# Pooled attention and a top-1 mixture of experts on one core: second products turned by TensorE for four parts, first V loads behind Q, later landings in the planner's model, one outer condition

## The chip, the cores and the metric

The kernel runs on one core of a Trainium2 chip. The core has five engines that run in parallel, each in its own order: TensorE (PE, matrix products and transposes), VectorE (DVE), ScalarE (ACT), GpSimd (POOL) and SyncE (SP, which here only issues transfers). Transfers run on DMA engines, and engines wait for one another and for transfers by semaphores. The metric is the time of one execution on the device in microseconds (us).

## The reference

```python
q_pool = q.reshape(B, H, S // 2, 2, D).mean(axis=3)
scores = scale * np.matmul(q_pool, k.transpose(0, 1, 3, 2))
attn = softmax(scores)
x = np.matmul(attn, v).transpose(0, 2, 1, 3).reshape(N, 512)

expert_idx = np.argmax(x @ w_gate, axis=1)
gate_w = softmax(x @ w_gate)[np.arange(N), expert_idx]
for e in range(8):
    mask = expert_idx == e
    h = np.maximum(x[mask] @ w1[e], 0.0)
    out[mask] = gate_w[mask, None] * (h @ w2[e])
```

The sizes are B = 8 batches, H = 8 heads, S = 1152 positions and D = 64 features a head, in fp32. Pooling leaves 576 rows of Q a batch, so N = 4608 tokens of 512 features go to the experts. w1 is 512 x 1024 for each expert and w2 is 1024 x 512. A token goes to one expert only.

## The kernel before, in words

**A planner.** `Flow` collects steps (`add`, an engine, a cost, a key, the steps it comes after, the buffers it holds) and `emit` simulates them once, when the program is built: a free engine takes the ready step with the smallest key. The key is a due time in units of the products; the constants `K_LOAD` to `K_SLOT` and `AHEAD` shift the keys of one kind of step. `carry` (L115 on) is a step that issues a transfer, together with a step on a modelled DMA that takes `move` ns, and `late` ns more until others may go on. These numbers change only the order. Each engine then executes in the order found; DVE, for instance, never lets a later instruction pass one that waits. Gathers and scatters are `paced`: such a transfer gets a dependence on PE's instruction before it in the order.

**Attention.** A batch is four pairs of heads. `load_pair` (L456) loads K, Q (two overlapping transfers) and V of a pair on SP (L472), pools Q (`qp`, L479, on POOL; for the very first pair on DVE) and turns K and Q on PE (L500, L506). `scores` (product L544) and `values` (L648) follow, with the exponent on ACT (L577). POOL adds the exponentials up in folds of 3.9 us (L623), and PE finishes the sums (L632). PE works in tile modes there (`ROWS`, `QUADS`, `COLS`), and changing the mode costs something. K, Q have one buffer each, V has three.

**Routing.** After each batch the router (L711 on) chooses experts; `enlist` (L825, POOL) scatters (token, weight) records to lists in memory, one per expert.

**The experts.** Tokens of an expert are worked on in 15 parts of 160 to 416 tokens: two early ones of 384 that start within the last batch, and those of `RANKS`, ordered by size of the expert. The parts of 288 tokens are r0's second and r4's first, those of 320 and of 416 are r3's first and r5. A part loads its list (`li`, L910, POOL), makes an index from it on DVE (`ix`, L920), gathers rows of x in blocks of 32 tokens (`xr`, `xq`, L926, POOL), weighs and turns them (`turn_tokens`: DVE L1083, L1084, L1087) and splits them in a high and a low half (`xh` on ACT L1091, `xl` on DVE L1046). Weights are split likewise (`w1h`, `w2h` on ACT L1108, `w1l`, `w2l` on DVE L1046). Every fp32 product is three fp32r products: high by high, low by high, high by low. `first_products` (L1140) leave the hidden rows turned (1024 features on partitions by tokens), in halves `hh` (ACT L1147) and `hl` (DVE L1149). In `second_products` hidden rows of a block of up to 128 tokens are stationary and w2 moves:

```python
for r in range(x.nr):
    for k, (a, b) in enumerate(((hh, wh), (hh, wl), (hl, wh))):
        made = nc.tensor.matmul(py.t[:n], a[:, c, hs], b[:, c % 2, :], ...)
```

That is 24 products of 512 columns for each block (L1170), whether it has 128 tokens or the last 32. ACT copies the block (L1188) and POOL scatters its rows to the output (L1178).

**The end.** Two conditions stand behind the planned part, each read by every engine from a small table on the core (`stab`): a fallback `If` (load L1263, branch L1265), which is taken only when a list overflows, and a loop over slots left over (load L1282, loop L1290), which has no pass for these inputs.

Of the kernel before, what the change touches and what calls it, by code (L numbers as in the profile page):

```python
# [42 lines left out]
K_FIRST = 29  # L43
K_PUT = 79
K_SPREAD = -1
K_NEXT = 38
TABLE_OPS = 3
K_TAB = 1
K_SLOT = 46
# [6 lines left out]
AHEAD = 216  # L56
# [209 lines left out]
def kernel(  # L266
# [148 lines left out]
    def open_attention(exact, base, pairs, units):  # L415
# [10 lines left out]
        o.turned = []  # L426
# [28 lines left out]
    def done(*steps):  # L455
        return [s for s in steps if s is not None]  # L456

    def load_pair(o, f, key, b, hp):
# [15 lines left out]
        q0 = f.carry("SP", 960, lambda: [load(qn.t[i * D:(i + 1) * D], qb[i * BL:i * BL + D]) for i in range(2)],  # L474
                     key + K_LOAD, (), [qn], 2600)
        x.v = f.carry("SP", 480, lambda: load(vn.t, heads(v, b, hp).rearrange("h (p c) d -> p h c d", p=P)),
                    key + (-30 if opening else K_V), (), [vn], 2600)
# [216 lines left out]
    def routing(o, f, key, b, xT, rec, sums, ready, hold=()):  # L694
# [144 lines left out]
        for j in range(NJ):  # L839
            outs.append(f.carry("POOL", 1230, lambda j=j: enlist(j), at + (K_PUT if b is None or b < B - 2 else 0) * j / NJ, done(p, *hold), [di, re], 40, 2400, paced=CALM))  # L840
# [49 lines left out]
    def tokens_of(o, f, key, tab, s, n, known, stored, early=False, m=None):  # L890
# [47 lines left out]
    def slot_table(o, f, key, ready, later=None):  # L938
# [81 lines left out]
        flush()  # L1020
        return known

    def flag(o, f, key, ready):
# [5 lines left out]
        for fn in (  # L1029
            lambda: nc.vector.tensor_reduce(f2, pm.t[0:1, :QP], axis=AX.X, op=ALU.max),  # L1030
            lambda: nc.vector.tensor_scalar(f3[:, 0:1], f2, 1.0, None, op0=ALU.is_le),
            lambda: nc.vector.tensor_scalar(stab[:, 1:2], f3[:, 0:1], -1.0, 1.0, op0=ALU.mult, op1=ALU.add),
        ):
            p = f.add("DVE", 100, fn, key, done(p), [pm])

# [119 lines left out]
    def second_products(o, m, f, x, key):  # L1155

        for r in range(x.nr):
            py = hold_of("py", lambda h: m.ps.tile([P, DM], F32, **h.own("py")))
# [4 lines left out]
            for c0 in range(0, NFC, 2):  # L1163
# [29 lines left out]
    with ExitStack() as cm, ExitStack() as units, ExitStack() as pairs:  # L1193
# [48 lines left out]
        for i, ns in enumerate(((EARLY_N,),) * EARLY + RANKS):  # L1242
# [3 lines left out]
            for j, n in enumerate(ns):  # L1246
# [7 lines left out]
                if j == 0:  # L1254
# [8 lines left out]
    again = nc.values_load(stab[0:1, 1:2], min_val=0, max_val=1,  # L1263
                           skip_runtime_bounds_check_because="a comparison's result")
    with tc.If(again > 0):  # L1265
        reset_state()
        empty_lists()
        with ExitStack() as cm:
            o = open_attention(True, cm, cm, cm)
            with tc.For_i(0, B, 1) as b:  # L1270
# [6 lines left out]
                for hp in range(NHP):  # L1277
                    attend(o, f, 0, b, hp, xT, sums, [])
# [47 lines left out]
```

## Time and profile before

| | before |
|---|---|
| median of three runs | 1222.98 us (1222.68 to 1224.88) |
| the profiled execution's own time | 1222.86 us |
| its span in the trace | 1221.3 us |
| mean granted clock of TensorE | 0.984 |
| busy: PE, weight loads | 1169.4 us (96%), 826.4 us (68%) |
| busy: DVE, ACT, POOL | 781.7, 629.7, 854.4 us |

The span is the time from the first to the last instruction in the trace; the execution's own time is taken around it. A busy engine is one whose instructions run; the time of instructions that issue, wait or branch does not count. The chain of waits follows the work that ended last back to the start. Attention takes about 12 to 735 us in the trace, the experts 735 to 1208, and the end the rest.

### The profile page before, as it was taken

The page shows a single profiled execution, that of the slowest core. Times are in us where ns is not written, and L with a number is a line of the kernel's source. Part 1 is how long each engine was busy: PE and PEld are TensorE (multiplying, and loading weights), DVE is VectorE, ACT ScalarE, POOL GpSimd, SP SyncE. Part 2 cuts the span into 40 slices and gives each one's busy share as a digit, 9 for nine tenths or more (in the row PEclk, how much of TensorE's full clock was granted, in tenths as well). Part 3 has the DMA queues.
Part 4 walks back from the last instruction along what each step waited for, and adds up shares of the span by engine and source line. Part 5 has one row for each costly group of instructions (what it writes and reads, how often), then busy time and mean ns, then how long its engine had stood idle before and what let it go on. Part 6 is the DMA issues. An engine that isn't in the chain of part 4 may idle for free.

```text
span 1221.3 us, 33596 instructions
## 1 busy us (share of the span) xinstructions
PE 1169.4 (96%) x14061; PEld 826.4 (68%) x14061; DVE 781.7 (64%) x2145; ACT 629.7 (52%) x768; POOL 854.4 (70%) x468
## 2 busy tenths in 40 slices
PE   7999999999999999999999998799999999999995
PEld 3555565566566566565665556688898888989784
DVE  5767777777777777778668658764546363636440
ACT  3676567666667567567666456341424141425340
POOL 2999899899899899899999153465666564630110
PEclk8999999999999999999999998899999998999998
DMA  7643333433523524524433315743434361615310
GB/s 196 157 119 88 103 104 88 123 95 96 124 84 102 126 77 112 126 83 113 109 93 117 108 48 169 184 141 96 130 118 141 104 187 37 193 45 185 121 63 19
DMA packets 76049, 138.10 MB, mean 113 GB/s; under 512 B 9833, under 2 KB 33265, under 8 KB 75888
## 3 DMA queue, kind: packets, MB, share of 16 engines
q1 hardware_dynamic: 65088, 116.18, 34.3%
q0 software_dynamic: 9712, 19.64, 5.5%
q8 instruction: 113, 1.85, 0.7%
q14 instruction: 48, 0.39, 0.1%
q10 hardware_dynamic: 1088, 0.03, 0.1%
HBM read 115.04 MB, written 21.02 MB: 111 GB/s over the span
## 4 chain that ended last, share of the span: by engine, by line
PE 78%; POOL 6%; DVE 5%; issue 4%; DMA 4%; ACT 2%; POOLq 0%; SPq 0%; DVEq 0%
PE st L544 19%; PE m L648 18%; PE py L1170 17%; PE ph L1140 15%; POOL fold L623 5%; PE sums L632 3%; DVE s L549 2%; PE st L500 2%; PE sums L618 1%; POOL lists L825 1%; ACT s L577 1%; DMA xr<-x_runs,ix 1%; PE st L506 1%; DMA lists<-re,di 1%; DMA xq<-x_runs,ix 1%
## 5 line engine op out<-in xcount | busy, mean ns | idle before, releaser
L549 DVE TENSOR_SCALAR_CACHE_REDUCE s<-st 128x576 f32<-128x576 f32 x576 | 421.0, 753 | 161.2 <-PE st L544 155.7
L577 ACT ACTIVATE s<-s,bias 128x1728 f32<-128x1728 f32 x192 | 321.4, 1730 | 177.9 <-DVE bias L573 156.4
L544 PE MATMUL st<-qT,kT 64*64 64x288 f32 x4608 | 372.3, 410 | 9.9 <-DVE s L549 6.7
L648 PE MATMUL m<-s,vn 64*64 64x288 f32 x4608 | 363.2, 405 | 0.0
L544 PEld LDWEIGHTS st<-qT,kT 64*64 64x64 f32 x4608 | 169.5, 133 | 140.0 <-DVE s L549 57.0
L648 PEld LDWEIGHTS m<-s,vn 64*64 64x64 f32 x4608 | 182.1, 133 | 84.6 <-ACT xT L653 2.6
L623 POOL TENSOR_TENSOR fold<-s 128x1728 f32<-128x1728 f32 x58 | 224.5, 3871 | 9.1 <-ACT s L577 8.4
L623 POOL TENSOR_TENSOR fold<-fold,s 128x1728 f32<-128x1728 f32 x58 | 224.9, 3877 | 1.6
L926 POOL DMA_INDIRECT xr<-x_runs,ix x99 | 113.8, 1149 | 91.5 <-PE ph L1140 24.5
L1140 PE MATMUL ph<-xh,w1h 128*128 128x384 f32 (+6 forms) x480 | 152.5, 318 | 17.8 <-DVE hl L1149 15.0
L1140 PE MATMUL ph<-xl,w1h 128*128 128x384 f32 (+6 forms) x480 | 151.0, 315 | 0.5 <-DVE xl L1046 0.5
L1140 PE MATMUL ph<-xh,w1l 128*128 128x384 f32 (+6 forms) x480 | 150.5, 313 | 0.0
L1178 POOL DMA_INDIRECT out_dram<-y,rec x41 | 45.7, 1114 | 143.7 <-PE py L1170 79.6
L1170 PE MATMUL py<-w2h,hh 128*128 128x512 f32 (+1 forms) x328 | 129.6, 395 | 0.0
L1170 PE MATMUL py<-w2h,hl 128*128 128x512 f32 (+1 forms) x328 | 129.3, 394 | 0.0
L1170 PE MATMUL py<-w2l,hh 128*128 128x512 f32 (+1 forms) x328 | 128.9, 393 | 0.0
L1147 ACT ACTIVATE hh<-ph 128x384 fp32r<-128x384 f32 (+5 forms) x100 | 48.7, 487 | 149.4 <-PE ph L1140 147.1
L1149 DVE SCALAR_TENSOR_TENSOR hl<-ph,hh 128x384 fp32r<-128x384 f32 (+5 forms) x100 | 54.6, 549 | 91.8 <-ACT hh L1147 91.7
L1140 PEld LDWEIGHTS ph<-xh,w1h 128*128 128x128 f32 x480 | 92.4, 193 | 22.0 <-DVE hl L1149 17.2
L1140 PEld LDWEIGHTS ph<-xl,w1h 128*128 128x128 f32 x480 | 92.3, 192 | 1.8 <-DVE xl L1046 0.9
L1140 PEld LDWEIGHTS ph<-xh,w1l 128*128 128x128 f32 x480 | 92.0, 192 | 0.0
L1188 ACT COPY y<-py 128x512 f32<-128x512 f32 (+3 forms) x41 | 24.0, 586 | 124.0 <-PE py L1170 114.7
(174 smaller groups left out, 1331.5 us busy)
## 6 DMA issues: line engine op xcount, KB each, us to landing
raw<-in_moe_w_dram SPq DMA_DIRECT2D x80, 512.0 KB
qn<-in_q_dram SPq DMA_DIRECT2D x64, 384.0 KB
kn<-in_k_dram SPq DMA_DIRECT2D x32, 576.0 KB
vn<-in_v_dram SPq DMA_DIRECT2D x32, 576.0 KB
x_runs<-row SPq DMA_DIRECT2D x24, 396.0 KB
xr<-x_runs,ix POOLq DMA_INDIRECT x99, 2.7
x_runs<-empty SPq DMA_DIRECT2D x4, 297.0 KB
xq<-x_runs,ix POOLq DMA_INDIRECT x49, 2.9
```

Source lines behind the costliest of these rows:

```text
L544: made = nc.tensor.matmul(pt.t[to, h, :HQ], x.kT.t[up, c * P + i * D:c * P + (i + 1) * D], x.qT.t[up, cols], start=True, stop=True, tile_p ...
L549: nc.vector.tensor_scalar(s.t[:, c], pt.t[:, :, :HQ], -SCALE, None, op0=ALU.mult, op1=ALU.min, accum_out=mx.t[:, c:c + 1],)
L577: nc.scalar.activation(s.t[:, c0:c0 + n], s.t[:, c0:c0 + n], AF.Exp, bias=bias.t, scale=-1.0)
L623: add = lambda to, a, b: nc.gpsimd.tensor_tensor(to, a, b, ALU.add)
L632: nc.tensor.matmul(sums.t[to, :HQ], ones4[:, hp, half, :], u.t[:, i, h], start=hp == half == 0, stop=hp == NHP - 1 and half == 1, tile_pos ...
L648: made = nc.tensor.matmul(pa[i].t[cs, :HQ], x.vn.t[up, h, c, :], s.t[up, c, h], start=c == 0, stop=c == NC - 1, tile_position=(up.start, c ...
L926: return nc.gpsimd.indirect_dma_start(out=x.xr[i // NQD].t[:, i % NQD, :], out_offset=None, in_=xg, in_offset=bass.IndirectOffsetOnAxis(ap ...
L1140: made = nc.tensor.matmul(view()[:, i, :], a[:, c, fp], b[:, c, :n], start=c == 0 and k == 0, stop=c == NDC - 1 and k == 2)
L1147: a = f.add("ACT", act(nb * n) - 44, lambda fs=fs, view=view: nc.scalar.activation(hidden(m)[0][:, fs, :n], view(), AF.Relu), at - 20, don ...
L1149: d = f.add("DVE", dve(nb * n), lambda fs=fs, view=view: nc.vector.scalar_tensor_tensor(hidden(m)[1][:, fs, :n], view(), 0.0, hidden(m)[0] ...
L1170: made = nc.tensor.matmul(py.t[:n], a[:, c, hs], b[:, c % 2, :], start=c == 0 and k == 0, stop=c == NFC - 1 and k == 2)
L1178: ins = nc.gpsimd.indirect_dma_start(out=out, out_offset=bass.IndirectOffsetOnAxis(ap=x.re.t[:up, r:r + 1], axis=0), in_=y.t[:up], in_offs ...
```

## The change

1. Fourteen constants of the planner are set anew.
2. The V loads of batch 0 get a dependence on both Q loads of their pair, so SP waits there until Q has landed. Later V loads come after the V load before them in the plan (a planner's rule alone).
3. The model lets the scatters of `enlist`, the loads of lists and the gathers land 2000 or 3000 ns later.
4. Parts with more than 256 tokens whose last block has 32 or 64 (288, 320, 288 and 416) take their second products the other way: a 128 x 128 piece of w2 is stationary and the hidden rows of all tokens move. The result is 4 groups of 128 output features by tokens; ACT copies each to `yT`, PE turns it back in 128 x 128 transposes (fp32, L1205 of the changed kernel), then ACT's copy and the scatter follow as before.
5. The two conditions at the end stand inside one outer `If`, on the sum of the flag and the slots (`stab[2]`), which two small instructions on DVE work out.

```diff
-K_LOAD = -65
-K_V = -40
-K_POOL = -16
-K_PIECE = -28
-K_TOP = -8
+K_LOAD = -57
+K_V = -36
+K_POOL = -7
+K_PIECE = -26
+K_TOP = -17
...
-K_EXP = 10
+K_EXP = 13
...
-K_ROW = 34
+K_ROW = 47
...
-K_FIRST = 29
-K_PUT = 79
-K_SPREAD = -1
-K_NEXT = 38
+K_FIRST = 37
+K_PUT = 88
+K_SPREAD = 4
+K_NEXT = 41
...
-K_TAB = 1
-K_SLOT = 46
+REST = (32, 64)
+K_TAB = 0
+K_SLOT = 45
...
-AHEAD = 216
+AHEAD = 270
...
+        first = not o.exact and b == 0
...
+        def load_v():
+            ins = load(vn.t, heads(v, b, hp).rearrange("h (p c) d -> p h c d", p=P))
+            if first:
+                for other in x.q_loads:
+                    tc.add_manual_dep(ins.ins, other.ins.name, mybir.DependencyInfo(
+                        mybir.DependencyClass.Sync, mybir.DependencyReason.DATA), reason="Q is needed sooner")
...
+        x.v = f.carry("SP", 480, load_v, key + (-30 if opening else K_V), done(q0) if first else done(o.before), [vn], 2600)
+        o.before = x.v
...
-            outs.append(f.carry("POOL", 1230, lambda j=j: enlist(j), at + (K_PUT if b is None or b < B - 2 else 0) * j / NJ, done(p, *hold), [di, re], 40, 2400, paced=CALM))
+            outs.append(f.carry("POOL", 1230, lambda j=j: enlist(j), at + (K_PUT if b is None or b < B - 2 else 0) * j / NJ, done(p, *hold), [di, re], 40, 4400, paced=CALM))
...
-        p = f.carry(at, 900 if early else 1100, load, key - LEAD, [*known, *stored], [x.re, x.li], 120, 9000 if early else 1000)
+        p = f.carry(at, 900 if early else 1100, load, key - LEAD, [*known, *stored], [x.re, x.li], 120, 9000 if early else 4000)
...
-        x.rows = done(*(f.carry("POOL", 1310, lambda i=i: gather(i), key + i * 3 / x.nb, done(p, *stored), [x.ix, x.xr[i // NQD]], 400, paced=CALM if early else CALM_X)
+        x.rows = done(*(f.carry("POOL", 1310, lambda i=i: gather(i), key + i * 3 / x.nb, done(p, *stored), [x.ix, x.xr[i // NQD]], 400, 2000, paced=CALM if early else CALM_X)
...
+        n, across = x.n, f.room is not None and x.n > 2 * P and x.of[-1] * BL in REST
+        if across:
+            yT = tile_of(o, "xT", [P, NHP, NQ])
+            turned = []
+            for d in range(NDC):
...
+                        for c in (c0, c0 + 1):
+                            for k, (a, b) in enumerate(((wh, hh), (wl, hh), (wh, hl))):
+                                made = nc.tensor.matmul(py.t[:, :n], a[:, c % 2, ds], b[:, c, :n],
+                                                        start=c == 0 and k == 0, stop=c == NFC - 1 and k == 2)
...
+                turned.append(f.add("ACT", act(n) - 44, lambda d=d, py=py: nc.scalar.copy(yT.t[:, d, :n], py.t[:, :n]),
+                                    at, done(p), [py, yT]))
...
+            if across:
+                def product(r=r, py=py, up=up):
+                    for d in range(NDC):
+                        made = nc.tensor.transpose(py.t[:up, d * P:(d + 1) * P], yT.t[:, d, r * P:r * P + up], ident)
+                    return made
+
+                p = f.add("PE", 60 * NDC, product, at + 40, turned, [py, yT])
...
+    some = nc.values_load(stab[0:1, 2:3], min_val=0, max_val=MAXS + 1,
+                          skip_runtime_bounds_check_because="a comparison's result and the sum of the slots")
+    with tc.If(some > 0):
```

The order of the instructions moves in many places. Three are shown, with the names of the programs (a number behind a name tells buffers apart).

First DVE, at the start of the parts of `RANKS`, around the index of the first list (`ix_2`, read from `li_2`); `hl` are the low halves of the hidden rows of the second early part. Before:

```order
L1046 TENSOR_TENSOR w2l1_10642<-raw_1_10439,w2h1_10641 128x1024
L920 TENSOR_SCALAR ix_2_10670<-li_2_10599,gid_147 128x12
L923 COPY rec2_2_10672<-li_2_10599 32x3 x4
L1046 TENSOR_TENSOR w2l2_10662<-raw_2_10557,w2h2_10661 128x1024
L1046 TENSOR_TENSOR w2l3_10694<-raw_3_10570,w2h3_10693 128x1024
L1149 SCALAR_TENSOR_TENSOR hl_10296<-ph_0_10677,hh_10295 128x384
```

and in the changed kernel, with the table of slots (L966, L1049) between:

```order
L1061 TENSOR_TENSOR w2l3_10681<-raw_3_10570,w2h3_10680 128x1024
L1046 TENSOR_SCALAR f3_221<-f3_221 1x1
L1164 SCALAR_TENSOR_TENSOR hl_10298<-ph_0_10671,hh_10297 128x384
L966 TENSOR_TENSOR t_rf_217<-t_rf_217,t_sT_218 1x25
L966 CAST stab_175<-t_cum_213 1x1
L1164 SCALAR_TENSOR_TENSOR hl_10298<-ph_1_10700,hh_10297 128x384
L932 TENSOR_SCALAR ix_2_10750<-li_2_10622,gid_147 128x12
L935 COPY rec2_2_10752<-li_2_10622 32x3 x4
```

The index moved from ahead of two weight halves and the first `hl` to behind the second.

Second DVE again, where the first ranked part (384 tokens) begins: its first block `xr_0` is weighed and turned, and the low halves of the expert's w2 are made beside it. Before:

```order
L1083 TENSOR_TENSOR xr_0_10910<-xr_0_10910,li_2_10599 128x4x4
L1084 TENSOR_TENSOR xr_0_10910<-xr_0_10910 128x4x128
L1087 STREAM_TRANSPOSE xt_0_11014<-xr_0_10910 128x4x4x32
L1046 TENSOR_TENSOR xl_10923<-xt_0_11014,xh_10922 128x4x128
L1046 TENSOR_TENSOR w2l0_11024<-raw_2_10708,w2h0_11023 128x1024
L1046 TENSOR_TENSOR w2l1_11038<-raw_3_10730,w2h1_11037 128x1024
L1046 TENSOR_TENSOR w2l2_11058<-raw_4_10796,w2h2_11057 128x1024
L1046 TENSOR_TENSOR w2l3_11076<-raw_5_10846,w2h3_11075 128x1024
L1149 SCALAR_TENSOR_TENSOR hl_10296<-ph_0_11063,hh_10295 128x384
```

and in the changed kernel:

```order
L1061 TENSOR_TENSOR w2l0_11018<-raw_2_10696,w2h0_11017 128x1024
L1061 TENSOR_TENSOR w2l1_11031<-raw_3_10715,w2h1_11030 128x1024
L1061 TENSOR_TENSOR w2l2_11046<-raw_4_10787,w2h2_11045 128x1024
L1098 TENSOR_TENSOR xr_0_10943<-xr_0_10943,li_2_10622 128x4x4
L1099 TENSOR_TENSOR xr_0_10943<-xr_0_10943 128x4x128
L1061 TENSOR_TENSOR w2l3_11057<-raw_5_10849,w2h3_11056 128x1024
L1102 STREAM_TRANSPOSE xt_0_11069<-xr_0_10943 128x4x4x32
L1061 TENSOR_TENSOR xl_10941<-xt_0_11069,xh_10940 128x4x128
L1098 TENSOR_TENSOR xr_1_11007<-xr_1_11007,li_3_10638 128x4x4
L1099 TENSOR_TENSOR xr_1_11007<-xr_1_11007 128x4x128
L1164 SCALAR_TENSOR_TENSOR hl_10298<-ph_0_11082,hh_10297 128x384
```

Three of the four weight halves moved from behind the weighing of `xr_0` to ahead of it, and the fourth between weighing and turning.

Third PE, at the end of the second products of r0's part of 288 tokens (`py` is the last of the four groups of output features, `m` the banks that take the transposes, `ph` the next part's first products). Before, after 24 products of one block came 24 of the next:

```order
L1170 MATMUL py_0_11599<-w2h3_11075,hh_10295 128x512
L1170 MATMUL py_0_11599<-w2l3_11076,hh_10295 128x512
L1170 MATMUL py_0_11599<-w2h3_11075,hl_10296 128x512
L1170 MATMUL py_1_11648<-w2h0_11023,hh_10295 128x512
L1170 MATMUL py_1_11648<-w2l0_11024,hh_10295 128x512
```

and in the changed kernel:

```order
L1186 MATMUL py_0_11680<-hh_10297,w2h3_11056 128x288
L1186 MATMUL py_0_11680<-hh_10297,w2l3_11057 128x288
L1186 MATMUL py_0_11680<-hl_10298,w2h3_11056 128x288
L1155 MATMUL ph_0_11720<-xh_11570,w1h0_11427 128x384
L1155 MATMUL ph_0_11720<-xl_11571,w1h0_11427 128x384
L1155 MATMUL ph_0_11720<-xh_11570,w1l0_11428 128x384
L1205 MATMUL m_0_11736<-ident_64,xT_0_11605 128x128 x4
L1205 MATMUL m_2_11744<-ident_64,xT_0_11605 128x128 x4
```

The products have 288 columns in place of 512; six first products of the next part stand between the last of them and the eight transposes of two blocks, and the third block's four follow later.

## Rows read from the trace of the kernel before

**Rows 1.** Windows: busy us (PE, PEld, DVE, ACT, POOL), clock, DMA share, GB/s

```profile
402.50:491.60 89.10, 87.69 (x1438) 53.95 (x1436) 66.62 (x200) 57.03 (x63) 85.24 (x35) 1.00 0.42 105
...
785.00:800.00 15.00, 9.43 (x45) 9.43 (x46) 12.21 (x42) 3.29 (x5) 8.04 (x7) 0.77 0.62 171
800.00:1000.00 200.00, 196.65 (x1064) 175.44 (x1063) 105.14 (x200) 70.04 (x110) 124.08 (x112) 1.00 0.42 125
```

**Rows 2.** Page: chain that ended last, shares of the span by line

```profile
PE st L544 19%; PE m L648 18%; PE py L1170 17%; PE ph L1140 15%; POOL fold L623 5%; PE sums L632 3%; DVE s L549 2%; PE st L500 2%; PE sums L618 1%; POOL lists L825 1%; ACT s L577 1%; DMA xr<-x_runs,ix 1%; PE st L506 1%; DMA lists<-re,di 1%; DMA xq<-x_runs,ix 1%
```

**Rows 3.** Chain of waits at the start: start us, us, what

```profile
2.27 7.34 DMA qn<-in_q_dram
...
12.52 3.41 PE st L544 x24
```

**Rows 4.** Transfers up to 9.6 us

```profile
DMA packets 1043, 1.82 MB, mean 190 GB/s; under 512 B 344, under 2 KB 344, under 8 KB 1042
```

**Rows 5.** Chain of waits in the batch from 402 us on

```profile
421.37 3.87 POOL fold L623
...
441.83 0.48 PE st L544 x8
...
444.17 0.65 PE st L544 x8
```

**Rows 6.** PE: timeline (start us, us, instruction); waits (us, times, longest)

```profile
790.57 0.69 PE L1140 MATMUL ph<-xh,w1h 128*128 128x384 f32 x1 [6.22 <-DVE hl L1149]
...
793.61 0.53 PE L1140 MATMUL ph<-xh,w1h 128*128 128x384 f32 x1
...
1010.24 0.63 PE L1140 MATMUL ph<-xh,w1h 128*128 128x320 f32 x1 [5.05 <-DVE hl L1149]
...
1015.47 0.47 PE L1140 MATMUL ph<-xl,w1h 128*128 128x320 f32 x1
...
PE ph L1140 <- DVE hl L1149: 15.0, 6, 6.2
```

**Rows 7.** Chain of waits, transfers ahead of PE's waits in the experts

```profile
769.14 10.20 DMA lists<-re,di
...
780.10 6.72 DMA li<-lists
...
823.95 5.30 DMA xr<-x_runs,ix
...
1001.53 7.22 DMA xr<-x_runs,ix
```

**Rows 8.** DVE's timeline, weighing to low half of one block of tokens

```profile
813.83 0.18 DVE L1083 TENSOR_TENSOR xr<-xr,li 128x16 f32<-128x16 f32 x1 [2.57 <-DMA xr<-x_runs,ix]
...
817.38 0.69 DVE L1046 TENSOR_TENSOR xl<-xt,xh 128x512 fp32r<-128x512 f32 x1 [1.91 <-ACT xh L1091]
```

**Rows 9.** Chain of waits, products of the experts one behind another

```profile
805.02 16.70 PE py L1170 x72
...
886.56 16.87 PE ph L1140 x96
...
920.13 11.41 PE ph L1140 x96
```

**Rows 10.** Transposes L730: timeline, and all of the line (ns minimum/median/maximum)

```profile
747.28 0.49 PE L730 MATMUL sums<-ident,sm 128*96 128x128 f32 x3
...
L730 PE MATMUL sums<-ident,sm x24: 270/273/315, 123.3 to 747.5; 128*96 128x128 f32 x24
```

**Rows 11.** POOL's end: last scatter; queue's instructions (ns; first, last start us)

```profile
1209.24 0.88 POOL L1178 DMA_INDIRECT out_dram<-y,rec  x1 [3.35 <-ACT y L1188]
...
L1282 POOLq TENSOR_LOAD <-stab x1: 302/302/302, 1211.7 to 1211.7; - x1
...
L1290 POOLq INC_SWDGE_SEM  x1: 1377/1377/1377, 1212.6 to 1212.6; - x1
...
L1321 POOLq DRAIN x3: 46/103/5052, 1215.4 to 1221.0; - x3
```

More of the change, by code (lines that the diff above doesn't have):

```diff
@@ L1020, in slot_table @@
         flush()
+        o.slots, o.counted = cum[:, NE - 1:NE], (last or [None])[0]
         return known
@@ L1032, in flag @@
             lambda: nc.vector.tensor_scalar(stab[:, 1:2], f3[:, 0:1], -1.0, 1.0, op0=ALU.mult, op1=ALU.add),
+            lambda: nc.vector.tensor_scalar(f3[:, 1:2], f3[:, 0:1], -1.0, 1.0, op0=ALU.mult, op1=ALU.add),
         ):
             p = f.add("DVE", 100, fn, key, done(p), [pm])
+        f.add("DVE", 100, lambda: nc.vector.tensor_tensor(stab[:, 2:3], f3[:, 1:2], o.slots, ALU.add), key, done(p, o.counted))
     def add_raw(m, cm, reuse):
@@ L1260 @@
         by_hand.close()
[L1263 to L1267, printed above, removed]
-        with ExitStack() as cm:
-            o = open_attention(True, cm, cm, cm)
-            with tc.For_i(0, B, 1) as b:
-                f = Flow()
-                xT = tile_of(o, "xT", [P, NHP, NQ])
-                rec = tile_of(o, "rec", [QP, 2, 3, H])
-                sm = tile_of(o, "sm", [P, HQ], bufs=1)
-                o.batch = b
-                sums = sum_bank(o)
-                for hp in range(NHP):
-                    attend(o, f, 0, b, hp, xT, sums, [])
-                row_sums(o, f, 0, sums, [], rec, sm, False)
-                routing(o, f, 0, None, xT, rec, sums, [])
-            slot_table(o, Flow(), 0, ())
@@ new lines @@
+    with tc.If(some > 0):
+        again = nc.values_load(stab[0:1, 1:2], min_val=0, max_val=1,
+                               skip_runtime_bounds_check_because="a comparison's result")
+        with tc.If(again > 0):
+            reset_state()
+            empty_lists()
+            with ExitStack() as cm:
+                o = open_attention(True, cm, cm, cm)
+                with tc.For_i(0, B, 1) as b:
+                    f = Flow()
+                    xT = tile_of(o, "xT", [P, NHP, NQ])
+                    rec = tile_of(o, "rec", [QP, 2, 3, H])
+                    sm = tile_of(o, "sm", [P, HQ], bufs=1)
+                    o.batch = b
+                    sums = sum_bank(o)
+                    for hp in range(NHP):
+                        attend(o, f, 0, b, hp, xT, sums, [])
+                    row_sums(o, f, 0, sums, [], rec, sm, False)
+                    routing(o, f, 0, None, xT, rec, sums, [])
+                slot_table(o, Flow(), 0, ())
+        last = nc.values_load(stab[0:1, 0:1], min_val=0, max_val=MAXS,
+                              skip_runtime_bounds_check_because="the sum of the slots")
+        with ExitStack() as cm:
+            o, m, f = Pools(), Pools(), Flow()
+            o.wk = cm.enter_context(tc.tile_pool(name="wk2", bufs=1))
+            o.ps_m = cm.enter_context(tc.tile_pool(name="ps_m2", bufs=2, space=PSUM))
+            add_raw(m, cm, "pool")
+            add_moe(m, cm, "pool")
+            with tc.For_i(0, last, 1) as s:
+                x = tokens_of(o, f, 0, rtab, s, T, (), ())
+                weights_of(m, f, x, 0, etab, s, ())
+                turn_tokens(o, m, f, x, 0)
+                x.w1, x.w1_ready = split_weights(m, f, x, "w1", 0, 0, 0)
+                x.w2, x.w2_ready = split_weights(m, f, x, "w2", 0, 0, 0)
+                first_products(o, m, f, x, 0)
+                second_products(o, m, f, x, 0)
```

40 lines of the change are left out of this document (17 added, 23 removed).

## The prediction

> **What bounds the kernel now.** I read the windows by stage first. In one batch of attention TensorE (PE) is busy 87.69 of 89.10 us and GpSimd (POOL) 85.24; in 200 us of the MoE PE is busy 196.65 us at the full granted clock, POOL 124.08, VectorE (DVE) 105.14, ScalarE (ACT) 70.04 [rows 1]. The chain of waits, read next, says the same by lines: PE's score product has 19%, the value product 18%, the second MoE product 17%, the first 15%; POOL's folds have 5% [rows 2]. So time goes where PE gets less to do (second products), where PE stands still (waits in the MoE, start, end), and in attention only if PE and POOL both get less, for both are nearly full. The profiled execution took 1222.86 us (span 1221.3), 0.12 us under the median of the runs; the sum is made against 1222.86 and stands for the median too. A measurement here tells about 0.2% from no change, 2.4 us.
>
> **Start.** The chain begins with the first Q load, 7.34 us from 2.27 us on; the first score product stands at 12.52 [rows 3]. By 9.6 us the DMA queues have moved 1.82 MB [rows 4], nearly all of it in the last 7.6 us, which is 240 GB/s; one K (0.59 MB) and one Q (two loads, 0.79 MB) are 1.38. The other 0.44 MB are V, or 1.8 us at that rate. With V behind Q's landing, Q lands about 1.8 us sooner. V is not late: values follow a whole pair of products later. Behind the waiting V on SP stand the next Q loads, whose buffer is in use until the pooling anyway. I take **-1.8** (bounds -2.3, the 0.44 MB at the mean of 190 GB/s [rows 4], and 0: Q may be bound by its own transfer). One rule speaks against it: by the Trainium skill (DMA: Bandwidth & Descriptors, Queues, rings and completion order) the descriptors of one ring start in order, so V issued behind Q on the same queue would not delay it, and the term would be 0. The 0.44 MB that moved before Q's end speak for overlap; no run here shows the order inside a ring.
>
> **Attention.** The constants only move steps. Counted in the two programs, PE changes its tile mode 226 times before and 248 after, because the pieces of the K transposes (L500) are split finer. Eight score products take 0.48 us inside a mode and 0.65 just behind a change [rows 5], so a change costs at most 0.17; I take 0.1: 22 x 0.1 = 2.2 us. Beside it: a batch has 89.1 - 87.69 = 1.4 us of idle PE, so over seven batches the new order can gain some 10 us at most, and lose as easily, since the fold chain on POOL (3.87 us a fold [rows 5]) stands in the chain of waits. I take **+2** (bounds -6 and +8).
>
> **The first wait of the MoE.** At 790.57 PE waited 6.22 us for the low half of the hidden rows (`hl`, DVE), and its next ten products of 384 columns began 0.338 us apart (3.04 us for nine steps [rows 6]), where 0.176 is usual (worked out below): 1.5 us more. The granted clock of the stretch from 785 to 800 was 0.77 [rows 1]; PE had stood idle and then ran at the lower level (1.2 GHz). Its cause is on DVE, in the first place of the order shown: the index of the first list (L920) stands ahead of two weight halves and of `hl`, and waits for the list, whose last scatter took 10.20 us and whose load took 6.72 [rows 7]. The change models these landings later (2400 to 4400, 1000 to 4000), and the index now stands behind both `hl`. What is left of the wait I put at 1.0: -6.7. But the second place takes it back. The last gather of the first ranked part now stands 7.0 us of PE's work ahead of the part's first product, before 11.2. A gather lands 5.3 to 7.2 us after its issue [rows 7]; from the weighing of a block to the end of its low half took 4.2 us (813.83 to 818.07 [rows 8]), all ahead of PE, and `w2l3` stands between them now. 9.5 to 11.4 us against 7.0 make a new wait of 2.5 to 4.4 us. I take 4.4 and 1.3 for the lower clock behind it: +5.7. Net **-1** (bounds -4.2, the short wait at full clock, and +2, a gather 3 us slower).
>
> **The later waits.** PE waited six times for `hl`, 15.0 us [rows 6]; without the first that is 8.8, of which 5.05 at 1010.24. `hl` stands there on DVE behind the weighing of a later part, whose gather had not landed: the chain has gathers of 5.30 and 7.22 us right ahead of these waits [rows 7]. From 1010.24 on nineteen steps of 320 columns took 5.23 us [rows 6], 0.275 each against 0.147 (below): 2.4 us more at the lower clock. Together 8.8 + 2.4 = 11.2. With 2000 ns more for each gather in the planner, the last gather now stands mostly 4.8 to 9.7 us of PE's work ahead of the weighing (before 2.6 to 5.0; counted by PE's instructions between the two places, at the trace's spacings), and up to three `hl` pass ahead of it. Most waits go; I keep 2.2 us for what comes in their place: **-9** (bounds -11.2 and -2).
>
> **The second products of four parts.** Before, parts of 288, 320, 288 and 416 tokens take 3 + 3 + 3 + 4 = 13 blocks of 24 products with 512 columns each: 72 take 16.70 us, 0.232 each, 13 x 24 x 0.232 = 72.4 us; a block with 32 tokens costs as much as a full one. Now each part takes 4 x 24 products with as many columns as it has tokens. The first products show such prices: 256 columns 11.41 us for 96, 384 16.87 (0.176 each) [rows 9]; on the line through them 288 costs 0.133, 320 0.147 and 416 0.190. 96 x (0.133 + 0.147 + 0.133 + 0.190) = 57.9. Saved: 14.5. Added: 13 blocks x 4 = 52 transposes. Three fp32 transposes in a row stood in 0.49 us (the last with its 0.27 us of duration [rows 10]), so about 0.11 us apart: 5.7 us. The sixteen copies on ACT lie beside PE, which goes on with the next group; only the last of each part is waited for. The third place of the order has six first products between (1.05 us), while the copy may stand behind a cast of weights on ACT: I put 0.5 us for the first part, 0.2 for the others, and 1.4 for some 13 changes of tile mode and a dearer change of weights, 2.5 us in all. Then each token block's copy and scatter are as before. -14.5 + 5.7 + 2.5 = **-6** (-6.3, rounded) (bounds -9 with no wait, and 0: transposes at their whole duration of 0.273 [rows 10], 14.2). The Trainium skill (TensorE: Matmul & The Clock Gate, Part 4: PE-mode transpose) gives some 275 ns for a 128x128 transpose in a kernel; by it the term would be about 0. The row's duration agrees with that figure, its spacing does not, and spacing is what PE pays. I take the spacing.
>
> **The end.** Behind the last scatter (1209.24, 0.88) POOL goes through two rounds: load a flag, branch, add to a semaphore of its queue. The second starts with its load at 1211.7 and reaches the drain at 1215.4; 1.38 of that is the semaphore [rows 11]. With one outer condition the round runs once: 3.7 us less, if the drain of 5.05 us runs from its own start. I take **-3.6** (bounds -3.7 and 0: if the drain ends by the scatter's landing, at the same moment as now).
>
> **Sum.** -1.8 + 2 - 1 - 9 - 6 - 3.6 = -19.4: 1222.86 - 19.4 = **1203.5 us**. The two additional operations of the flag on DVE (under 0.1 us each) stand beside a waiting DVE and cost nothing.
>
> **Rivals.**
> 1. *The transposes cost their duration*, with longer waits for `yT`: -6 becomes +0.5, the sum -13: 1210. For it: they are fp32, and their durations. Against it: the spacing [rows 10]. Chance 0.14.
> 2. *The later landings do not help*, as the waits move to other parts (as at the first ranked part): -9 becomes -2, the first wait +2: about 1213.5. For it: DVE remains in order, and only a planner's number changes. Against it: the chain names the gathers [rows 7], and the wider distances answer to them. Chance 0.10.
> 3. *Attention becomes slower than before*, one mechanism: pooling Q on POOL is due later (K_POOL -16 to -7), the folds stand ahead of it, and each pair's Q transposes, so its scores, start late, which PE, with 1.4 us of reserve per batch, cannot cover. From 3.1 us per batch on (seven batches) the other 19.4 us plus 2.4 are lost; at one fold of 3.87 us: 7 x 3.87 = 27, 1230. For it: POOL's 85.24 of 89.10. Against it: four poolings a batch still stand in a queue with the same work. Chance 0.09.
> 4. *The first wait goes and does not come back*, and attention gains 4 us: 1203.5 - 5.7 - 6 = 1192. For it: gathers may land in 5 us, and the constants may fit the new order. Chance 0.17.
> 5. *The end stays*, fixed by the drain: 1207. And *the wait of V does nothing*, as Q is bound by its own transfer: 1205. Neither changes a sign; both lie in the forecast's case.
>
> **Chances and range.** My forecast, with the two of 5, has 0.46; 1 has 0.14, 2 0.10, 3 0.09, 4 0.17; 0.04 stay for sums of bad bounds near 1222. Faster by over 2.4 us: all but 3 and three quarters of the rest, 0.88; within 2.4 us 0.03; slower 0.09. The range from 1192 to 1216 takes in 4 at its lower end, 1, 2 and the bounds of single terms (attention +8 gives 1209.5, with transposes at full price 1215.5), and leaves out 3 and the sums of bad bounds.
>
> **What would show it.** Right: the first score product at about 10.7 us; the batches at 89 us; in the MoE few idle times of PE over 1 us, but one of 3 to 6 us at the first ranked part; transposes about 0.11 us apart; 3.6 us less between the last scatter and the end. Wrong: batches of over 92 us, or waits for `hl` of more than 6 us in all behind the first ranked part; transposes 0.27 us apart; a drain that ends as late after the scatter as now.

## The result, and the profile after

The changed kernel took 1211.13 us, the median of 4 runs (1210.62 to 1211.85), against 1222.83 for the kernel before: a ratio of 0.9902, 95% interval 0.9888 to 0.9916, so 12.0 us less, where 19.4 were forecast. The sign and the range (1192 to 1216) hold; the size is 0.6 of what was said. Its profiled execution took 1210.88 us, with a span of 1209.1.

Four stretches divide a span: from the start to the first score product; attention from there to the end of the last value product; the experts from there to the start of the last product; and the end. The columns "before" and "after" are of the two profiled executions, against which the prediction's terms can be held. The table's fourth row begins a little later than the fourth stretch, at the last scatter; the stretch itself is also 1.9 us shorter.

| | before | after | difference | forecast |
|---|---|---|---|---|
| first score product at | 12.52 | 12.77 | +0.25 | -1.8 |
| attention | 722.46 | 727.30 | +4.8 | +2 |
| experts | 472.93 | 457.60 | -15.3 | -16 |
| last scatter to the end of the span | 12.06 | 10.15 | -1.9 | -3.6 |
| span | 1221.30 | 1209.15 | -12.15 | -19.4 |

The experts gave what was forecast, the other three stretches did not. That the experts' sum fits is luck: terms inside it were off in opposite directions. PE's waits there show two of them (us in total, times, longest), where [rows 6] has 15.0 us in six waits for `hl`:

```profile
PE ph L1155 <- ACT xh L1106: 6.0, 2, 4.3
PE ph L1155 <- DVE hl L1164: 4.6, 2, 4.2
```

Six waits for `hl` became two, and a new one for `xh`, 4.3 us long, has come. The chain of waits (start us, us, what) shows the longest wait for `hl`, which ends at 794.32 and answers to the wait of 6.22 at 790.57 in [rows 6]:

```profile
777.98 13.39 DMA raw<-in_moe_w_dram
...
791.44 1.05 ACT w2h L1123
...
792.52 1.23 DVE w2l L1061
...
793.80 0.47 DVE hl L1164
...
794.32 5.75 PE ph L1155 x24
```

The list and its index are gone from this place ([rows 7]); a load of w2 stands there, 13.39 us from issue to landing, and ACT's cast and DVE's low half of it are ahead of `hl`. The 24 products behind it took 5.75 us, 0.240 each in place of 0.176, so PE was at the lower clock again (granted clock 0.75 from 794.32 to 800.07), 1.5 us.

The same load was no cause before. There the last of these casts was done at 783.5 (ACT's timeline), 3.3 us before the index could begin (DVE's timeline):

```profile
782.46 1.05 ACT L1108 CAST w2h<-raw 128x1024 fp32r<-128x1024 f32 x1 [0.94 <-DMA raw<-in_moe_w_dram]
```

```profile
786.84 0.23 DVE L920 TENSOR_SCALAR ix<-li,gid 128x12 int32<-128x12 int32 x1 [6.70 <-DMA li<-lists]
```

That load was issued at 772.17, so 10.3 us before its cast; in the changed kernel it is 13.5 us (777.98 to 791.44). The load itself has become slower. Three traces with the order of before have 9.5 to 10.3 us here, five with the order of after 13.5 to 15.1.

The wait for `xh`, in the chain of waits again, at the first ranked part:

```profile
823.91 1.06 ACT w2h L1123
...
826.13 0.18 DVE xr L1098
...
826.95 1.22 DVE w2l L1061
828.17 0.63 DVE xt L1102
...
828.82 0.63 ACT xh L1106
...
829.47 0.78 DVE xl L1061
...
830.29 1.97 PE ph L1155 x5
```

No gather is in it: weighing (`xr`, 826.13) comes behind the low halves of w2, which come behind ACT's casts, and one more (`w2l`, 826.95) stands between weighing and turning. PE waited 4.27 us and then ran the part's first products at a granted clock of 0.53, as a window from 829 to 835 us has it (columns as in [rows 1]):

```profile
829.00:835.00 6.00, 5.39 (x16) 5.00 (x17) 1.84 (x4) 0.93 (x2) 1.75 (x3) 0.53 0.58 193
```

The second products and the transposes, in the chain (288, 320 and 416 columns; 8 and 12 transposes):

```profile
879.70 12.00 PE py L1186 x90
...
892.76 0.87 PE m L1205 x8
...
1018.53 13.97 PE py L1186 x96
...
1124.36 18.13 PE py L1186 x96
...
1143.45 1.31 PE m L1205 x12
```

That is 0.133, 0.146 and 0.189 us a product and 0.109 a transpose, and PE waited nowhere for `yT`. The duration of a transpose is 0.273 as in [rows 10]:

```profile
L1205 PE MATMUL m<-ident,xT x52: 270/273/273, 892.6 to 1145.9; 128*128 128x128 f32 x36, 128*32 128x128 f32 x12, 128*64 128x128 f32 x4
```

The end on POOL (ns minimum/median/maximum, first and last start in us), to be held against [rows 11]; its last scatter starts at 1199.00:

```profile
L1311 POOLq EVENT_SEMAPHORE  x6: 17/30/1681, 1199.6 to 1200.1; - x6
...
L1311 POOLq INC_SWDGE_SEM  x1: 1420/1420/1420, 1201.8 to 1201.8; - x1
...
L1370 POOLq DRAIN  x3: 50/103/5050, 1203.3 to 1208.9; - x3
```

One round is gone, but one of the six semaphore steps of the other now takes 1.681 us. It waits for two semaphores, of which one is the last scatter's; it is met 2.8 us behind the scatter's start. Before, POOL came to that semaphore only 3.3 us behind the scatter and did not wait. So the drain now starts 4.3 us behind the scatter's start. Before, it was 6.2, and 3.7 less would have been 2.5.

### The profile page after: what moved, and what is told of

Read it like the earlier page. It is cut to its first block, busy times and chain, and to the rows that moved or that the text cites. A ratio compares the mean times of both kernels' runs of the same rounds, so it can differ in the third digit from the quotient of the medians.

```text
span 1209.1 us, 33797 instructions
## 1 busy us (share of the span) xinstructions
PE 1162.4 (96%) x14185; PEld 820.3 (68%) x14185; DVE 784.1 (65%) x2147; ACT 636.5 (53%) x784; POOL 848.2 (70%) x468
## 4 chain that ended last, share of the span: by engine, by line
PE 46%; DVE 4%; issue 3%; POOL 3%; DMA 2%; ACT 1%; POOLq 0%; DVEq 0%; ACTq 0%; SPq 0%
PE ph L1155 16%; PE py L1216 10%; PE m L660 6%; PE st L556 5%; PE py L1186 5%; POOL fold L635 2%; DVE s L561 1%; PE sums L630 1%; DMA raw<-in_moe_w_dram 1%; ACT s L589 1%; PE sums L644 1%; POOL lists L837 1%; DMA xr<-x_runs,ix 1%; PE m L1205 0%; DVE w1l L1061 0%
## 5 line engine op out<-in xcount | busy, mean ns | idle before, releaser
L556 PE MATMUL st<-qT,kT 64*64 64x288 f32 x4608 | 365.1, 412 | 9.0 <-DVE s L561 7.3
L660 PE MATMUL m<-s,vn 64*64 64x288 f32 x4608 | 355.4, 405 | 0.0
L556 PEld LDWEIGHTS st<-qT,kT 64*64 64x64 f32 x4608 | 162.1, 133 | 147.7 <-DVE s L561 61.8
L660 PEld LDWEIGHTS m<-s,vn 64*64 64x64 f32 x4608 | 174.4, 133 | 86.1 <-issue 2.6
L938 POOL DMA_INDIRECT xr<-x_runs,ix x99 | 109.4, 1105 | 92.9 <-PE st L556 24.9
L1155 PE MATMUL ph<-xh,w1h 128*128 128x384 f32 (+6 forms) x480 | 152.9, 318 | 10.8 <-ACT xh L1106 6.0
L1216 PE MATMUL py<-w2h,hh 128*128 128x512 f32 x224 | 88.6, 396 | 0.0
L1216 PE MATMUL py<-w2h,hl 128*128 128x512 f32 x224 | 88.4, 394 | 0.0
L1216 PE MATMUL py<-w2l,hh 128*128 128x512 f32 x224 | 88.1, 393 | 0.0
L837 POOL DMA_INDIRECT lists<-re,di x48 | 46.3, 964 | 51.9 <-PE m L660 18.8
```

What stands on the lines that cost most here:

```text
L556: made = nc.tensor.matmul(pt.t[to, h, :HQ], x.kT.t[up, c * P + i * D:c * P + (i + 1) * D], x.qT.t[up, cols], start=True, stop=True, tile_p ...
L660: made = nc.tensor.matmul(pa[i].t[cs, :HQ], x.vn.t[up, h, c, :], s.t[up, c, h], start=c == 0, stop=c == NC - 1, tile_position=(up.start, c ...
L837: ins = nc.gpsimd.indirect_dma_start(out=lists, out_offset=bass.IndirectOffsetOnAxis(ap=di.t[:, j:j + 1], axis=0), in_=re.t[:, j, :], in_o ...
L938: return nc.gpsimd.indirect_dma_start(out=x.xr[i // NQD].t[:, i % NQD, :], out_offset=None, in_=xg, in_offset=bass.IndirectOffsetOnAxis(ap ...
L1155: made = nc.tensor.matmul(view()[:, i, :], a[:, c, fp], b[:, c, :n], start=c == 0 and k == 0, stop=c == NDC - 1 and k == 2)
```

## The experiments

Each ratio is against the kernel before, run beside it. Chips differ by some us, so the stretches of the traces are compared too; each trace is of one execution.

| kernel | time (its range) | before | ratio, 95% interval | first score | attention | experts | scatter to end |
|---|---|---|---|---|---|---|---|
| after, V without wait | 1214.09 (1213.07 to 1216.75) | 1226.08 | 0.9905, 0.9891 to 0.9919 | 12.75 | 727.57 | 459.39 | 10.22 |
| after, gate's weights later | 1217.88 (1216.45 to 1219.27) | 1226.08 | 0.9927, 0.9914 to 0.9940 | 12.55 | 731.11 | 461.37 | 10.17 |
| after, two conditions | 1217.40 (1215.29 to 1218.41) | 1226.08 | 0.9927, 0.9914 to 0.9940 | 12.64 | 728.28 | 459.10 | 12.06 |
| after, tokens turned first | 1209.40 (1209.04 to 1209.74) | 1226.08 | 0.9859, 0.9844 to 0.9875 | 13.27 | 728.14 | 454.97 | 10.17 |
| before, turned products alone | 1211.70 (1210.08 to 1213.96) | 1227.94 | 0.9862, 0.9839 to 0.9885 | 13.23 | 727.90 | 457.15 | 12.07 |
| after, old landings | 1213.44 (1211.67 to 1215.14) | 1227.94 | 0.9874, 0.9853 to 0.9895 | 13.24 | 731.26 | 457.00 | 10.31 |
| after, old attention constants | 1217.75 (1215.94 to 1219.20) | 1227.94 | 0.9916, 0.9899 to 0.9934 | 12.74 | 735.37 | 454.86 | 9.87 |
| after, w2 modelled later | 1212.09 (1211.70 to 1212.12) | 1227.94 | 0.9867, 0.9848 to 0.9886 | 12.59 | 731.26 | 455.15 | 10.13 |
| before again | 1224.46 (1222.28 to 1226.35) | 1223.57 | 1.0003, 0.9994 to 1.0013 | 13.12 | 722.74 | 474.60 | 12.06 |
| after again | 1212.96 (1210.49 to 1214.12) | 1223.57 | 0.9910, 0.9896 to 0.9925 | 12.91 | 727.41 | 459.62 | 10.06 |
| before, later landings alone | 1219.55 (1218.61 to 1219.97) | 1223.57 | 0.9969, 0.9956 to 0.9983 | 13.22 | 724.38 | 466.07 | 12.05 |
| the combination | 1201.33 (1200.06 to 1201.73) | 1223.57 | 0.9817, 0.9804 to 0.9830 | 13.92 | 724.66 | 448.93 | 10.22 |

The first four ran on one chip, the next four on a second, the last four on a third.

**The start: V without its wait.**

```diff
-            if first:
-                for other in x.q_loads:
-                    tc.add_manual_dep(ins.ins, other.ins.name, ...)
```

> The changed kernel without the dependence of the first V loads on Q; the order on every engine is the same. Theory (the wait buys nothing): Q's landing is held up by other work than V, the first score product stays within 0.5 us of 12.77 and the time within 1.5 us of the changed kernel's. Rival (the bytes of V ahead of Q's end cost Q time, and only the early K load spoiled it): without the wait the first score product comes 1 to 2 us later than 12.77 and the time is 1 to 2 us longer.

The first score product stood at 12.75 us, as with the wait. The wait buys nothing. This does not test V's place, though: without the wait V is issued at 8.18 us, behind K's next load at 7.73, and not at 2.91 as in the kernel before. For V's place there are only traces of whole kernels. Five with V at 2.9 us have the first score product at 12.52 to 13.92 (median 13.22), nine with V later at 12.55 to 13.27 (median 12.75). So the +0.25 above lies in the spread of executions; a gain of some tenths is not excluded, one of 1.8 us is not seen. Since K's next load had come into V's place, the next run took away other traffic.

**The start: gate's weights off ACT's queue.**

```diff
-            nc.scalar.dma_start(out=wg[s * D:(s + 1) * D, :, half, ...], in_=wg_src[s])
+                nc.sync.dma_start(out=wg[s * D:(s + 1) * D, :, half, ...], in_=wg_src[s])
...
+                    f.carry("SP", 2400, load_gate, 1, outs, [], 900)
```

> The changed kernel with the four loads of the gate's weights (wg, 1088 packets under 512 B) moved from ACT's queue at the start to SP, behind the first pairs. Theory (the small packets of wg took the DMA time that V left free): Q lands 1 to 2 us sooner, the first score product at about 11 to 11.8 us instead of 12.77, the time 1 to 1.5 us shorter. Rival (Q is bound by its own transfer): first score product within 0.3 us of 12.77, time the same.

Up to 9.6 us 48 packets under 512 B moved in place of 1136, and yet the first score product came at 12.55, 0.2 us sooner. That theory falls too. What holds Q until 9.7 us, its own transfer or K's beside it, was not tried. Attention took 731 us, 3 us more than in the other three kernels on this chip. SP's order has four more loads among those of the first batch; that they are the cause was not shown.

**The end: two conditions again.** The tail of before, word for word, in the changed kernel.

> The changed kernel with the two separate conditions of before at its end; nothing else differs. Theory (the removed round had covered the landing of the last scatter, which POOL now waits for with 1.68 us): the end from the last scatter to the end of the span is 12.06 us as before instead of 10.03, the time 2.0 us longer. Rival (a whole round, as forecast): 3.6 us longer.

From the last scatter to the end 12.06 us, where the changed kernel has 10.15: the outer condition is worth 1.9 us, not 3.6. In this kernel's trace the drain starts at 1207.5, 6.2 us behind the scatter's 1201.35, and its second round waits for nothing:

```profile
L1336 POOLq EVENT_SEMAPHORE  x17: 17/43/43, 1204.3 to 1207.3; - x17
```

The whole time, a ratio of 0.9927 against the changed kernel's 0.9902, is longer by some 3 us, but the two intervals overlap; the stretch is the measurement.

**The first ranked part: tokens before weights.**

```diff
-    def split_weights(m, f, x, kind, key, step, pool_bits):
+    def split_weights(m, f, x, kind, key, step, pool_bits, after=()):
...
-                      key + step * j, done(got[j]), [raw[j], w[j]])
+                      key + step * j, [*done(got[j]), *after], [raw[j], w[j]])
...
-                    w.w2, w.w2_ready = split_weights(m, f, w, "w2", at, 10, 0)
+                    w.w2, w.w2_ready = split_weights(m, f, w, "w2", at, 10, 0, x.turned if i == EARLY else ())
```

> The changed kernel with w2's casts of the first ranked expert due only after its first part's tokens are turned. On PE 12 rows of the order differ, on DVE 48. Theory (the wait of 4.27 us at 829.49 comes from DVE's order, where weighing stands behind w2l0 to w2l2, which wait for PE to release w2): the wait falls to about 1 us, the lower clock behind it (2.2 us) goes too, and the time is 4 to 6 us shorter, if no weight is late for the second products. Rival (the gathers land late, as the prediction had it): the wait stays above 3 us and the time within 1.5 us.

PE's wait at this part fell to 1.24 us and another of 0.28, the experts to 454.97, against 459 to 461 in the three other kernels on that chip; the time is 4.7 us less than that of the changed kernel without V's wait. The wait was DVE's order, and what is left of it is a gather, which is now in the chain of this kernel, a copy of ACT and the cast behind it:

```profile
827.04 2.53 DMA xr<-x_runs,ix
...
829.64 0.59 ACT y L1234
830.22 0.53 ACT xh L1106
...
830.77 0.70 DVE xl L1061
...
831.52 2.54 PE ph L1155 x13
```

**The first wait: w2 modelled later.**

```diff
-            key + 60 + j, after, [x.raw2[j]], 2300) for j in range(4)]
+            key + 60 + j, after, [x.raw2[j]], 2300, getattr(x, "late2", 0)) for j in range(4)]
...
+            w.late2 = 10000 if i == 1 else 0
```

> The changed kernel in which the planner takes the four w2 loads of the second early part to land 10000 ns later; PE's order is the same, on DVE 20 rows move, and two hl pass ahead of the casts of these weights. Theory (the wait of 4.21 us at 794.32 is now for w2's landing, 13.39 us after its issue, which DVE and ACT have ahead of hl): the wait falls below 2 us, the lower clock behind it (1.5 us) goes, the time is 3 to 6 us shorter. Rival (the list is as late as the weights, so the index behind the second hl holds the third): a wait of 3 us or more stays, a few products later, and the time within 2 us.

PE's order is that of the changed kernel, row by row. The wait of 4.2 us became two, of 1.14 and 0.70 (PE's timeline):

```profile
800.65 0.44 PE L1155 MATMUL ph<-xh,w1h 128*128 128x384 f32 x1 [1.14 <-DVE hl L1164]
805.84 0.45 PE L1155 MATMUL ph<-xh,w1h 128*128 128x384 f32 x1 [0.70 <-DVE hl L1164]
```

The experts took 455.15 (457.60 and 459.62 in the changed kernel, on other chips). So w2's landing ahead of `hl` was the cause in the changed kernel. The list, due at nearly the same time, holds DVE only a little (0.18 and 0.76 us). This edit only moves the casts out of the way; what makes the load some 3 us slower in the new plan was not tried.

**The turned products alone.** The changed `second_products` in the kernel before, and nothing else.

> The kernel before with the turned second products of the four parts alone. Theory (a transpose costs its spacing of 0.11 us, the second products 0.133 to 0.19 a column group): 14.5 - 5.7 = 8.8 us less of PE's work in the experts, so 7 to 9 us less in all, if the waits for hl stay as they are. Rival (a transpose costs its duration of 0.27 us, or the waits for yT are long): 0 to 2 us less.

More than expected: the experts fell to 457.15, 15.8 to 17.5 us less than the two traces of the kernel before (472.93, 474.60), of which 8.8 are PE's work by the prices above. The rest are mostly waits and the lower clock behind them. PE waited for `hl` three times, 8.1 us, and not six times, though no landing was changed:

```profile
PE ph L1141 <- DVE hl L1150: 8.1, 3, 5.0
```

The plan behind the changed parts is another one. Where PE waited 5.05 us at 1010.24 [rows 6], three more `hl` stand ahead of the weighing on DVE in this trace, and PE waited 0.49. Neither theory of this run had that.

**The old landings in the changed kernel.**

```diff
-[di, re], 40, 4400, paced=CALM)
+[di, re], 40, 2400, paced=CALM)
-9000 if early else 4000)
+9000 if early else 1000)
-x.xr[i // NQD]], 400, 2000, paced=CALM if early else CALM_X)
+x.xr[i // NQD]], 400, paced=CALM if early else CALM_X)
```

> The changed kernel with the landings of before in the planner's model (2400, 1000, 0). Theory (the later landings took the waits for hl away): PE's waits for hl behind the first ranked part come back, 6 to 11 us in all with the lower clock, and the experts take 6 to 11 us more than the 457.6 us of the changed kernel. Rival (the other constants, AHEAD above all, did it): the waits stay below 2 us, the experts within 2 us of 457.6, less if the wait of 4.27 us at the first ranked part goes.

The experts took 457.00 us, no more than with the later landings. The waits behind the first ranked part came back to 2.4 us in all (0.43 in the changed kernel, 1.04 in its second trace below). At that part the wait of 4.27 us for `xh` is gone, and one of 2.47 for `hl` has come. In the changed kernel the landings give back at the first ranked part what they gain later.

**The later landings alone,** the reverse edit in the kernel before.

> The kernel before with the later landings (4400, 4000, 2000) alone. Theory (the landings take the waits for hl away, as the prediction had it): PE's waits in the experts fall from 18 to 10 us or less and the experts take 8 to 11 us less. Rival (the waits went with any new plan, and the landings give as much at the first ranked part as they take later): waits above 14 us, the experts within 4 us of the kernel before's.

The experts took 466.07 us, 8.5 less than the kernel before on the same chip, and PE waited 3.7 us for `hl` in place of 13.8. So the theory holds for this kernel. Here, too, the slower load of w2 has taken the list's place at the first wait (3.5 us); the chain has

```profile
773.78 12.64 DMA raw<-in_moe_w_dram
```

where the kernel before on this chip has at most 10.2 us from the same issue to the cast. The new wait of 4.3 us for `xh` at the first ranked part is here too:

```profile
PE ph L1140 <- ACT xh L1091: 6.9, 2, 4.3
PE ph L1140 <- DVE hl L1149: 3.7, 2, 3.5
```

The landings and the turned products take away mostly the same later waits for `hl`: of some 9 us the landings alone leave 0.2, the turned products alone 3.1.

**Old constants of attention in the changed kernel:** the nine that the expectation names, set as before.

> The changed kernel with nine constants of attention (K_LOAD, K_V, K_POOL, K_PIECE, K_TOP, K_EXP, K_ROW, K_SPREAD, K_NEXT) as before, the rest as changed. Theory (these constants made attention 4.8 us longer): from the first score product to the last value product it takes 722 to 724 us instead of 727.3, and the time is 3 to 5 us shorter if the experts stay at 457.6. Rival (the order around the routing, from K_FIRST, K_PUT and the later landings, made it longer): attention stays above 726 us.

Attention took 735.37 us, longer, not shorter. The 727.3 is of another chip; on this one the changed kernel's order of attention took 731.26 (the run with w2 modelled later), so the old constants cost 4.1 us here. In the experts the load of w2 took at most 8.9 us again, PE's first wait fell to 0.65 us, and they took 454.86. In attention the old constants do not bring the old length back: V's rule, `K_FIRST`, `K_PUT` and the landings of the changed kernel stand beside them here. Which of the constants and rules makes attention longer stays open.

**Both kernels again on one chip.**

> The kernel before itself, for its trace on the chip of the next three. On another chip the kernel before had attention in 722.5 us, and the same order of PE (the run with the turned products alone) took 727.9 on this call's or another chip, so attention's length differs by chip. Expected: attention 722 to 729 us here, the experts 472 to 474, the time of the kernel before. Two theories of the 15.8 us that the experts lost with the turned products alone: they are true (experts here 472 to 474), or a part is the chip (465 or less).

> The changed kernel itself, beside the kernel before on one chip. Theory (the change's order of attention is longer, not the chip): attention from the first score product on is 3 to 5 us longer than in the kernel before, the experts 15 us shorter, the end 1.9 us. Rival (the chip): attention within 1.5 us of the kernel before.

Attention took 722.74 us in the kernel before and 727.41 in the changed one: the order makes it 4.7 us longer, not the chip. PE's waits between 12 and 735 us for VectorE, ACT and POOL there grew from 11.9 to 14.5 us. Those for folds and copies grew by 4.3, those for DVE fell by 2; the rows that changed most, in the kernel before, then in the changed one:

```profile
PE sums L632 <- POOL fold L623: 0.9, 5, 0.2
```

```profile
PE sums L742 <- ACT sm L756: 2.9, 4, 0.9
PE sums L644 <- POOL fold L635: 2.9, 6, 1.3
```

The other 2 us are as much as the 22 more changes of tile mode cost at 0.1 us each; that was not measured by itself. Two more traces of this chip divide the 4.7 us: the later landings alone give 724.38 (+1.6), and the combination below, which has them but neither the constants nor V's rule, 724.66. So a good half of it comes with parts 1 and 2 of the change.

**The combination.** The kernel before with parts 3 to 5 of the change, the two edits above (tokens before weights, w2 modelled later), and without parts 1 and 2.

> The kernel before with the turned second products, the later landings and the one outer condition, but with the constants and the V loads of before, the four w2 loads of the second early part modelled 10000 ns later, and w2's casts of the first ranked expert due after its first part's tokens are turned. Theory (the sum of what the runs so far showed): attention as in the kernel before, the experts at 450 to 454 us, the end 10.1 us, 22 to 26 us less than the kernel before and 8 to 12 less than the changed kernel. Rival (each new plan brings new waits of its own in place of the old): experts at 457 or more, 16 to 19 us less.

1201.33 us, 22.4 us less than the kernel before (a ratio of 0.9817) and 11.6 less than the changed kernel on the same chip. Experts 448.93, attention 724.66, end 10.22. Its waits for `hl` are these:

```profile
PE ph L1144 <- DVE hl L1153: 2.2, 2, 1.5
```

## Why the prediction was right in sign and too large

The forecast was 1203.5, the profiled execution 1210.88: 7.4 us apart. By its own steps:

- **Start, -1.8: not seen, +0.25** in this pair of executions, which is within their spread. The step was "the other 0.44 MB are V ... Q lands about 1.8 us sooner". The 0.44 MB were counted up to 9.6 us. Q's last packet had ended by 8.7 us, when 1.56 MB had moved, so at most 0.18 MB of V were ahead of it. Without them Q's last packet also ended at 8.7 us. The bound of 0 was the right end, up to some tenths. By the Trainium skill (DMA: Bandwidth & Descriptors, Queues, rings and completion order) the descriptors of one ring start in order, by which V behind Q would not hold Q up and the term would be 0. The traces are nearer to that than to 1.8 us, but none shows the order inside a ring.
- **Attention, +2: +4.8,** inside the bounds. The term for changes of tile mode is of the size of what is left when the waits are taken off; that the new order adds 2.6 us of waits, more for folds and copies and less for DVE, was allowed for only in the bound.
- **The first wait, -1: wrong, +4.5.** Before, it cost 6.2 + 1.5. After, the wait at 794 cost 4.2 + 1.5 and the first ranked part 4.3 + 2.2 (95 products in 18.92 us, where 0.176 each make 16.7). "What is left of the wait I put at 1.0" is the step that failed. It holds only if w2 is there as early as before. With the cast at 782.46, its low half and `hl` (1.05 + 1.2 + 0.5 us) end at about 785.2, and PE stood idle from 784.35, so some 0.9 us would indeed have been left. In the changed kernel PE's idle time began at 790.10, and w2 landed only at 791.37, after 13.39 us. The prediction had no term for a transfer that the new plan makes slower; what slows it stays open: with the later landings alone it is slow as well, with the old constants of attention it is not. The new wait at the first ranked part was forecast at 4.4 us and measured 4.27, but for a wrong reason: not the gather's landing, but weighing put behind w2's low halves, which "tokens before weights" showed.
- **The later waits, -9: -10.8** (8.8 + 2.4 became 0.43). The size holds, the reason only in part. The later landings alone do it in the kernel before. In the changed kernel the old landings leave 4.9 us of these waits, but they spare the 4.27 us for `xh`, and the experts come out the same. The turned products' new plan takes most of these waits away as well, which the prediction did not have. So part of the fit is luck.
- **The second products, -6: -8.8.** Product and transpose were priced rightly (57.9 us forecast; 0.133, 0.146 and 0.189 measured; 0.11 against 0.109). The 2.5 us for waits and changes of mode did not show: PE never waited for `yT`, and the sum below leaves little room for them. A transpose lasts 0.273 us, but eight in a row start 0.109 apart, so they overlap and PE pays 0.109. The Trainium skill (TensorE: Matmul & The Clock Gate, Part 4: PE-mode transpose) has some 275 ns for a 128x128 transpose in a kernel's context, where it speaks of bf16; the duration of these fp32 ones agrees. Rival 1 falls.
- **The end, -3.6: -1.9.** "The round runs once: 3.7 us less" overlooked that the removed round had hidden the last scatter's landing. With the round gone, POOL comes to the scatter's semaphore 1.68 us too early. The step was priced by what it takes, and not by what is late next.

The sum of these terms is 0.25 + 4.8 + 4.5 - 10.8 - 8.8 - 1.9 = -12.0, and the spans differ by 12.15. Inside the experts the first wait was 5.5 us worse than forecast, the later waits and the products 1.8 and 2.8 better, so that -15.3 against -16 is right by cancelling. Rival 2 (the waits move to other parts) described one place of the experts, not all of them. Rival 3 (attention) has the right sign and a fifth of its size; its mechanism was not tested.

## What to carry to other kernels

Where a wait ends with one transfer, look for what is due just behind it: the end gave 1.9 us in place of 3.7 because the scatter's landing came next. And do not take the other transfers' times from the old order: the first wait came back because the load of w2, in time before, took 13.4 us in place of some 10 in the new plan. Where a planner writes the order, an edit's gain is not the sum of its parts: turned products alone took the experts down by nearly twice their work, and two edits that each removed the same waits did not add up. Read DVE's order at the place itself, since moving w2's casts behind the tokens gave some 4 us there.

## What was not expected of the hardware

The same order of every engine in attention took 722.5 us in the first trace and 722.7 on the chip of the last four runs, but 727.9 on the chip of the four before (the kernel with the turned products alone, whose attention is that of the kernel before). The changed kernel's order says the same: 727.4 on the one, 731.3 on the other. The kernel before had medians of 1226, 1228 and 1224 us on the three chips. What differs was not found, and each is one trace. So terms of a few us are told only from traces of one chip.

Taking away the wait of V, or a thousand small packets, did not move the first score product by more than some 0.2 us. And the same load of 512 KB landed some 10 us after its issue in one plan and 13 to 15 us in another.
